# Moving mask making and two memsets on GpSimd, one first-layer group ahead of the first turn, and a fourth relu tile

## The chip, the cores and the metric

The kernel runs on one core of one Trainium2 chip. The metric is the device time of one execution in microseconds, as the median of several runs. The core has five engines with queues of their own: TensorE (PE, with its weight loads as PEld), VectorE (DVE), ScalarE (ACT), GpSimd (POOL) and SyncE (SP), which here issues the transfers.

## The reference

Sliding-window attention over q, k, v of shape (8, 8, 576, 64), then a two-layer feed-forward with a squared relu:

```python
scores = (q @ k.T) / sqrt(64); masked to |i - j| <= 32
attn = softmax(scores) @ v                       # (8, 8, 576, 64)
x = attn.transpose(0, 2, 1, 3).reshape(4608, 512)
r = max(x @ w_in, 0)                             # w_in  (512, 2048)
out = (s * r * r + b) @ w_out                    # w_out (2048, 512)
```

All inputs and the output are float32.

## The kernel before

The kernel interleaves attention, batch by batch, with the feed-forward, token block by token block. It casts to bf16 on the way in and multiplies in bf16.

**Order.** Nothing is issued in the order of the source. Each `add(...)` makes a task with an engine, an estimated cost, what it reads and writes, and a key. `plan()` then goes through a simulated schedule and always takes the task that can start first by the estimates, ties going to the lower key and then to the one created earlier. `emit()` writes the engines' queues in that order, with semaphore waits. On the chip each queue runs strictly in that order. The source order still counts, since a ring's tile is handed out in the order of creation, and so fixes who waits for whom.

**Start.** Batch 0's q and k come by pairs of heads into the eight staging tiles `STG` (`load_pair`, L662), are cast to bf16 (`cast_qk`, L687), turned by TensorE into one of the two PSUM banks `W` (`turn_pair`, L700), and copied out as `qt` (ACT, L705) and `kt` (DVE, L706). GpSimd makes the identity and `NEG`, an additive band that opens batch 0's score banks (`opened`, L957), with `affine_select` (`band`, L482 and L487).

**Weights.** `w_in` and `w_out` come in eight tiles each through the same `STG` ring (L550) and are cast by GpSimd (L553). The loads of batch 1's q and k reuse the ring behind the `w_out` tiles, so SP issues each of them when a `w_out` cast is done.

**Masks.** Batches from 1 on multiply the exponentials by `MASK` (L987, L838). `masks()` makes it with four `affine_select`s, then makes three variants from it, each a copy (L517) and one or two memsets (L520), used from batch 3 on. `colsum()` needs two tiles set beforehand (L1180, L1181); it forms the column sums of `w_out` for the term with b (TensorE L1182, DVE L1186, TensorE L1189, DVE L1191).

**First layer.** Token blocks 0, 1 and 2 have 96, 256 and 160 tokens. Their first layer is cut into groups (block, quarter of the 2048 hidden columns). `s1` runs a group into a `W` bank (L1119), ACT applies relu into one of `NR1` tiles `R1` (L1126), DVE squares it into `GT` (L1128). A group of block 0 takes one bank, a group of blocks 1 or 2 takes two, in turn. `FIRST` orders the groups and the four `TURN`s, in each of which one pair of heads of batch 1 is turned through the same two banks and its scores are issued. The last turn also brings the remaining rows and the first unit of batch 1.

**Second layer.** `early()` runs the second layer of the first four 128-token tiles in pieces as hidden columns become ready (L1168); later tiles run in `s2` (L1137). DVE forms the output (L1153), SP stores it.

Of the kernel before, what the change touches and what calls it, by code (L numbers as in the profile page):

```python
# [19 lines left out]
NUNIT = (NTILE + 1) // 2  # L20
# [10 lines left out]
WINE = ("pool", "pool", "pool", "pool")  # L31
TURNKEY = -17.5
TURN = (None, 0)
FIRST = ((0, 0), (1, 0), (0, 1), (1, 1), (2, 0), (2, 1), (0, 2), (1, 2), (2, 2), TURN, (0, 3), TURN, (1, 3), TURN, (2, 3), TURN)
WOUTE = (("pool", "pool"),) * 4
TAIL = ("act", "dve")
HOST = (("k", 3), ("q", 0))
# [289 lines left out]
def bass_sliding_window_symmetric__then__act_starrelu_kernel(  # L327
# [23 lines left out]
    with ExitStack() as es:  # L351
# [16 lines left out]
            uid["n"] += 1  # L368
            return es.enter_context(nc.psum_tensor(f"{nm}_{uid['n']}", list(shape), dt))

        NSTG, NNAT, NEX, NXN, NR1, NOUT, XR = 8, 6, 5, 5, 3, 5, 2048
        WIN_BF = sb((128, 4, DFF), BF16, "win")
        WOUT_BF = sb((128, 16, DM), BF16, "wout")
        XT = sb((128, NPAIR, XR), BF16, "xt")
# [14 lines left out]
        MASK = MASKS[0]  # L389
# [7 lines left out]
        ONESW = sb((128, 128), BF16, "onesw")  # L397
# [5 lines left out]
        OUTS = [sb((128, DM), F32, "outs") for _ in range(NOUT)]  # L403
# [17 lines left out]
        g = _Graph(queues)  # L421
        add = g.add
# [27 lines left out]
        def number(c, u):  # L450
            return c * NUNIT + u
# [41 lines left out]
        band(IDENT[:, :], ONESW[:, :], "IDENT", 0, 0, -98)  # L493
        for p0 in (0, 64):
            band(NEG[p0:p0 + 64, :], NEG[p0:p0 + 64, :], ("NEG", p0), 0, 64, -97, -FAR, source=("NEG", p0))
        ones = ONESW.rearrange("p (one c) -> p one c", one=1).to_broadcast((128, 4, 128))
        add("pe", [lambda e: e.matmul(W[:, 1, :].rearrange("p (a c) -> p a c", a=4), lhsT=ONESW[:, :], rhs=ones,
                                      start=True, stop=True)] * WARM,
# [12 lines left out]

        def masks(after):

            for p0 in (0, 64):
                band(MASK[p0:p0 + 64, :], ONESW[p0:p0 + 64, :], ("MASK", 0, p0), 0, 64, -24.0, waits=[after])
            for i, cuts in ((1, ((0, 96), (64, 0))), (2, ((64, 96),)), (3, ((0, 0),))):
                add("pool", lambda e, i=i: e.tensor_copy(MASKS[i][:, :], MASK[:, :]), 250,  # L517
                    reads=[("MASK", 0, 0), ("MASK", 0, 64)], writes=[("MASK", i, 0), ("MASK", i, 64)], key=0.0)
                for p0, c0 in cuts:
                    add("pool", lambda e, i=i, p0=p0, c0=c0: e.memset(MASKS[i][p0:p0 + 64, c0:c0 + WIN], 0.0), 150,  # L520
                        writes=[("MASK", i, p0)], key=0.0)
        for i in range(2):
            for c0 in (0, WIN + S):
                zero("dve", QT[i][:, :, c0:c0 + WIN], ("QTZ", i, c0), 150, key=-98 if i == 0 else -20)
            add("dve", lambda e, i=i: e.memset(VB[:, i * NUNIT:i * NUNIT + NUNIT, :, :].rearrange("p t h c -> p (t h) c")[:, :, D:D + 1], 1.0), 150,
                writes=[("VBO", i)], key=-57 if i == 0 else -20)
# [3 lines left out]
        land = {}  # L530
# [53 lines left out]
        def cast_v(c, u, key, eng, slack):  # L584
            vs, vb, n = number(c, u) % NUNIT, number(c, u) % (2 * NUNIT), 64 * len(tiles(c, u))
            add(eng, (lambda e: e.copy(VB[0:n, vb, :, 0:D], VST[0:n, vs, :, :])) if eng == "act" else
                (lambda e: e.tensor_copy(VB[0:n, vb, :, 0:D], VST[0:n, vs, :, :])),  # L587
                {"act": 617.0, "dve": 420.0, "pool": 750.0}[eng],
                reads=[("VST", vs)], writes=[("V", vb, y) for y in (0, 1)], key=key, slack=slack)

        def load_rows(y, load_key):

# [426 lines left out]
        def attention():  # L1019
            seq = {"k": -200.0}  # L1020

            def nxt():
                seq["k"] += 1.0
                return seq["k"]

            def w(which, i):
                for x in (0, 1):
                    load_weights(which, i, x, nxt(), WINE[i] if which == "in" else WOUTE[i][x])

            for pr in range(NPAIR):  # L1030
                for name in "qk":
                    load_pair(0, name, pr, nxt())
                    turn_pair(0, name, pr, -60.0 + 0.1 * pr, banks, K0[pr] if name == "k" else Q0[pr], 200.0)
                pair_scores(0, pr)
            pick()
            for name, t in ORDER0:
                if name == "v":
                    load_tail(nxt())
                elif name == "r":
                    load_rows(t, nxt())  # L1040
                elif name == "e":
                    load_rest(0, nxt(), REST[0], -26.5, 200.0)
                else:
                    w("in", t)
            place_v()
            turn_rest(0, -23.9, banks)
            place_tail()
            last_scores(0)
            first_units()
            masks(land["av", 0, NUNIT - 1])  # L1050
            for i, src in enumerate((moe_s, moe_b)):
                add("sp", lambda e, i=i, src=src: e.dma_start(SROW[0:128:32, i:i + 1], src.partition_broadcast(4)),
                    600.0, writes=[("SROW", i)], dma=("l", 1, 15.0), key=nxt())
            add("dve", lambda e: e.stream_shuffle(SB128[:, :], SROW[:, :], [0] * 32), 150,
                reads=[("SROW", 0), ("SROW", 1)], writes=[("SB128", 0), ("SB128", 1)], key=P2[0] - 8.0, slack=500.0)
            for step in ORDER1:
                if step[0] == "w":
                    w("out", step[1])
                elif step[0] == "v":
                    load_v(1, step[1], nxt(), "sp", [land["rows", y] for y in (0, 1)])  # L1060
                    cast_v(1, step[1], due(1, 0) - 4.0 + step[1], EV1[step[1]], 800.0)
                elif step[0] == "e":
                    load_rest(1, nxt(), REST[1], due(1, 0) - 1.4, 500.0)
                else:
                    for name in "qk":
                        load_pair(1, name, step[1], nxt())
            yield S
            for pr in range(NPAIR):
                if pr:
                    yield S  # L1070
                for name in "qk":
                    turn_pair(1, name, pr, TURNKEY + 0.1 * pr, banks, "dve" if name == "k" else "pool", 500.0)
                pair_scores(1, pr)
            turn_rest(1, due(1, 0) - 1.4, banks)
            last_scores(1)
            for u in range(NUNIT):
                last.append((1, u))
                close()
                yield closed[0]
            for b in range(PAIRS, B):  # L1080
                c = seq_of(b)
                later(b, due(c, group_of(b)[0]) - 24.0)
                for i, u in enumerate(group_of(b)):
                    load_v(c, u, due(c, u) - 35.0, late(b), [paced(b, PACEV[min(b, 4) - 2][i])])
                    cast_v(c, u, due(c, u) - 4.0, EV2[i], SLACK[3])
                for u in group_of(b):
                    unit(c, u)
                    yield closed[0]
            if seq_tiles(LONG) % 2 == 0:
                unit(LONG, seq_units(LONG) - 1)  # L1090
            while last:
                close()
            yield T
# [81 lines left out]

        def colsum():

            even, block = OUTS[NOUT - 2][:, 0:128], OUTS[NOUT - 1][:, :]
            made = [land["av", 0, NUNIT - 1]]
            add("pool", lambda e: e.memset(even, 1.0 / 32), 150, writes=[("OUTS", NOUT - 2)], key=-19.0, waits=made)  # L1180
            add("pool", lambda e: e.memset(block, 0.0), 500, writes=[("OUTS", NOUT - 1)], key=-19.0, waits=made)  # L1181
            add("pe", [lambda e, fc=fc, x=x: e.matmul(  # L1182
                SC[32 * x:32 * x + 32, 0, 0:128], lhsT=ONESW[:, 0:32], rhs=WOUT_BF[:, fc, 128 * x:128 * x + 128],
                start=(fc == 0), stop=(fc == 15)) for fc in range(16) for x in range(4)],
                1100, reads=["ONESW"] + [("Wout", i, x) for i in range(4) for x in (0, 1)], writes=[("SC", 0)], key=-12.0)
            add("dve", [lambda e, x=x: e.tensor_copy(block[32 * x:32 * x + 32, 128 * x:128 * x + 128],  # L1186
                                                     SC[32 * x:32 * x + 32, 0, 0:128]) for x in range(4)],
                800, reads=[("SC", 0)], writes=[("OUTS", NOUT - 1)], key=-12.0)
            add("pe", lambda e: e.matmul(SC[:, 1, :], lhsT=even, rhs=block, start=True, stop=True),  # L1189
                950, reads=[("OUTS", NOUT - 2), ("OUTS", NOUT - 1)], writes=[("SC", 1)], key=-12.0)  # L1190
            add("dve", lambda e: e.tensor_scalar(CVEC[:, :], SC[:, 1, :], SB128[:, 1:2], None, ALU.mult),  # L1191
                680, reads=[("SC", 1), ("SB128", 1)], writes=[("CVEC", x) for x in (0, 1)], key=P2[0])

        units, made = attention(), 0
# [5 lines left out]

        made = next(units)
        colsum()
        for m, i in FIRST:
            if m is None:
                made = next(units)
# [268 lines left out]
```

## Time and profile before

| what | value |
|---|---|
| time, median of 3 runs | 316.41 us (315.55 to 317.66) |
| profiled execution | 318.05 us, span 316.3 us |
| mean granted TensorE clock | 0.987 |
| TensorE busy | 303.9 us of the span |
| VectorE, ScalarE, GpSimd busy | 194.8, 141.9, 91.7 us |
| HBM read, written | 36.70 MB, 9.44 MB |

The span is the part of the profiled execution between its first and its last instruction; the rest of its time lies around it. The busy time of an engine says what it did, not whether anyone waited for it. For that one reads a stretch of the span by itself, and in it the wait that ended last.

### The profile page before, as it was taken

How to read it: one execution, taken by the hardware profiler on the slowest of the kernel's cores; microseconds unless marked ns; L12 is line 12 of the kernel's file. 1: busy time of each engine (PE TensorE's matmuls, PEld its weight loads, DVE VectorE, ACT ScalarE, POOL GpSimd, SP SyncE). 2: the span in 40 equal slices, each digit the busy share in tenths (PEclk: the TensorE clock that was granted, in tenths of full speed). 3: DMA queues.
4: the chain of work that ended last, by engine and by line, in shares of the span. 5: the costliest groups of instructions: out<-in, count | busy, mean ns of one | idle time of the engine just before them, and what ended most of it. 6: DMA issues, size and time to landing. Idle time of an engine off the chain costs nothing.

```text
span 316.3 us, 7961 instructions
## 1 busy us (share of the span) xinstructions
PE 303.9 (96%) x3348; PEld 161.6 (51%) x3348; DVE 194.8 (62%) x387; ACT 141.9 (45%) x224; POOL 91.7 (29%) x110
## 2 busy tenths in 40 slices
PE   6888969999999999999999999999999999999995
PEld 2466656567664454544444444444444444444444
DVE  4666465895897897795577576967445543333312
ACT  4746326356544775654265435444444333333300
POOL 3468973670406136131513411451000000000000
PEclk9799979999999999999999999999999999999999
DMA  6999999998994998799799799996221110000022
GB/s 214 330 380 388 360 229 241 225 188 296 248 182 137 297 166 164 242 206 153 184 290 151 149 251 313 167 169 157 64 63 51 52 46 33 35 35 33 36 96 74
DMA packets 100055, 56.10 MB, mean 177 GB/s; under 512 B 72048, under 2 KB 91248, under 8 KB 100016
## 3 DMA queue, kind: packets, MB, share of 16 engines
q1 hardware_dynamic: 100016, 55.56, 73.0%
q8 instruction: 27, 0.44, 0.6%
q14 instruction: 12, 0.10, 0.1%
HBM read 36.70 MB, written 9.44 MB: 146 GB/s over the span
## 4 chain that ended last, share of the span: by engine, by line
PE 83%; DMA 5%; POOL 4%; SPq 3%; DVE 3%; issue 1%; POOLq 0%
PE w L1119 36%; PE o L1137 35%; PE avn L864 4%; DMA stg<-in_moe_w_in_dram 4%; POOL wout L553 3%; PE sc L806 2%; DMA stg<-in_v_dram 1%; PE avn L1168 1%; SPq L662 1%; PE o L1168 1%; DVE outs L1153 1%; PE w L700 1%; PE avn L897 1%; SPq L673 1%; DVE vb L587 1%
## 5 line engine op out<-in xcount | busy, mean ns | idle before, releaser
L1119 PE MATMUL w<-xt,win 128*128 128x512 bf16 (+3 forms) x768 | 144.8, 327 | 1.1 <-issue 0.6
L1126 ACT ACTIVATE r<-w 128x512 bf16<-128x512 f32 (+2 forms) x148 | 86.6, 586 | 104.0 <-PE w L1119 87.6
L1137 PE MATMUL o<-wout,gt 128*128 128x512 bf16 (+1 forms) x528 | 126.8, 373 | 0.3 <-DVE gt L1128 0.3
L1128 DVE TENSOR_TENSOR gt<-r 128x512 bf16<-128x512 bf16 (+2 forms) x148 | 77.2, 526 | 75.9 <-ACT r L1126 75.5
L1119 PEld LDWEIGHTS w<-xt,win 128*128 128x128 bf16 x768 | 67.7, 98 | 53.9 <-issue 0.8
L1137 PEld LDWEIGHTS o<-wout,gt 128*128 128x128 bf16 x528 | 50.7, 98 | 55.8 <-DVE gt L1128 0.6
L755 POOL CAST nat<-stg 128x1024 bf16<-128x1024 f32 (+1 forms) x21 | 26.6, 1265 | 64.4 <-DMA stg<-in_q_dram 42.5
L772 POOL COPY kt<-ktr 128x512 bf16<-128x512 bf16 (+1 forms) x30 | 31.1, 1037 | 37.4 <-DMA ktr<-nat 35.9
L834 ACT ACTIVATE ex<-sc 128x1024 bf16<-128x1024 f32 (+1 forms) x28 | 28.6, 1023 | 22.5 <-PE avn L864 21.7
L1153 DVE SCALAR_TENSOR_TENSOR outs<-o,sb,cvec 128x512 f32<-128x512 f32 (+1 forms) x35 | 25.4, 728 | 11.4 <-PE o L1137 11.3
L890 DVE TENSOR_TENSOR xn<-avn,rec 128x512 bf16<-128x512 f32 (+1 forms) x31 | 21.3, 688 | 1.0 <-DVE rec L888 0.2
L838 DVE TENSOR_TENSOR ex<-ex,mask 128x1024 bf16<-128x1024 bf16 (+1 forms) x28 | 21.2, 757 | 1.1 <-ACT ex L834 0.5
L864 PE MATMUL avn<-vb,ex 64*64 64x65 bf16 x944 | 19.9, 197 | 0.3
L864 PEld LDWEIGHTS avn<-vb,ex 64*64 64x64 bf16 x944 | 12.9, 106 | 13.2 <-issue 7.8
L755 DVE CAST nat<-stg 128x1024 bf16<-128x1024 f32 (+1 forms) x15 | 12.2, 810 | 3.7 <-DMA stg<-in_k_dram 1.9
L587 DVE CAST vb<-vst 128x512 bf16<-128x512 f32 (+1 forms) x28 | 13.8, 494 | 0.8 <-DMA vst<-in_v_dram 0.7
L888 DVE RECIPROCAL rec<-avn 128x8 f32<-128x8 f32 (+1 forms) x31 | 6.2, 201 | 8.3 <-PE avn L864 8.0
L806 PE MATMUL sc<-qt,kt 64*64 64x128 bf16 x432 | 11.3, 216 | 0.0
L700 PE MATMUL w<-ident,nat 128*128 128x128 bf16 x64 | 7.0, 253 | 3.9 <-POOL nat L687 3.4
L905 ACT COPY xt<-avn 128x512 bf16<-128x512 bf16 (+2 forms) x14 | 7.1, 516 | 6.3 <-PE avn L897 6.3
L705 ACT COPY qt<-w 128x512 bf16<-128x512 bf16 x8 | 4.7, 584 | 11.3 <-PE w L700 11.3
L553 POOL CAST win<-stg 128x1024 bf16<-128x1024 f32 x8 | 8.6, 1080 | 3.6 <-DMA stg<-in_moe_w_in_dram 3.4
(119 smaller groups left out, 156.8 us busy)
## 6 DMA issues: line engine op xcount, KB each, us to landing
out_dram<-outs SPq DMA_DIRECT2D x35, 256.0 KB, 2.6
vst<-in_v_dram SPq DMA_DIRECT2D x28, 256.0 KB, 4.4
stg<-in_k_dram SPq DMA_DIRECT2D x6, 1024.0 KB, 10.6
stg<-in_q_dram SPq DMA_DIRECT2D x6, 1024.0 KB, 6.4
stg<-in_moe_w_in_dram SPq DMA_DIRECT2D x8, 512.0 KB, 9.3
stg<-in_moe_w_out_dram SPq DMA_DIRECT2D x8, 512.0 KB, 10.3
stg<-in_q_dram SPq DMA_DIRECT2D x8, 256.0 KB, 5.3
stg<-in_k_dram SPq DMA_DIRECT2D x8, 256.0 KB, 5.1
```

The source lines that it names most:

```text
L553: add(eng, (lambda e: e.copy(dst, stg)) if eng == "act" else (lambda e: e.tensor_copy(dst, stg)), {"act": 1040.0, "dve": 690.0, "pool": 11 ...
L755: add(eng, lambda e, x=x: e.tensor_copy(nat[0:top, 1024 * x:1024 * x + 1024].rearrange("p (i h d) -> p h i d", h=H, i=2), stg[0:top, :].re ...
L772: add("pool", lambda e, c=c, w=w: e.tensor_copy(KT[slot][:, :, c:c + w].rearrange("p a (s i) -> p a s i", i=4), KTR[slot][:, :, :, c // 4: ...
L834: add("act", lambda e, dst=flat_dst, src=flat_src: e.activation(dst, src, AF.Exp, bias=0.0, scale=0.125), 190 + 0.833 * 512 * len(hs), rea ...
L838: add("dve", lambda e, flat=flat, mask=mask: e.tensor_tensor(flat, flat, mask, ALU.mult), 130 + 0.53 * 512 * len(hs), reads=[("E", ei, hp, ...
L864: return [lambda e: e.matmul(av[64 * x:64 * x + 64, h, 0:D + 1], lhsT=buf[64 * g:64 * g + 64, h % 2, h // 2, c:c + 64], rhs=VB[64 * g:64 * ...
L890: add("dve", lambda e: e.tensor_tensor(XN[xi][0:p1, :].rearrange("p (a c) -> p a c", a=H), av[0:p1, :, 0:D], REC[ri][0:p1, :].rearrange("p ...
L1119: add("pe", [lambda e, g=g, kc=kc: e.matmul(wt[:, g, :], lhsT=WIN_BF[:, kc, (f0 + g) * 128:(f0 + g + 1) * 128], rhs=XT[:, kc, t0 % XR:t0 % ...
L1126: add("act", lambda e: e.activation(rt, wt, AF.Relu, bias=0.0, scale=1.0), 190 + 0.833 * ng * nt, reads=[("W", wb)], writes=[("R1", rb)], ...
L1128: add("dve", lambda e: e.tensor_tensor(GT[gs][:, f0:f0 + ng, g0:g0 + nt], rt, rt, ALU.mult), 130 + 0.53 * ng * nt, reads=[("R1", rb)], wri ...
L1137: add("pe", [lambda e, fc=fc: e.matmul(O[:, ob, 0:cn], lhsT=GT[gs][:, fc, g0:g0 + 128], rhs=WOUT_BF[:, fc, c0:c0 + cn], start=(fc == 0), s ...
L1153: add("dve", lambda e: e.scalar_tensor_tensor(OUTS[us][:, 0:cn], bank, SB128[:, 0:1], CVEC[:, c0:c0 + cn], ALU.mult, ALU.add), 200 + 1.07 ...
```

## The change

The four selects that make `MASK` and the two memsets of `colsum()` no longer wait for batch 0's last attention unit; they get keys that put them right behind `NEG`, at the start of the kernel. The three variants of the mask now wait for the last V cast of batch 1. In `FIRST`, group (0, 3) stands ahead of the first turn, and so each later group stands one turn earlier, with turns 2 and 3 together at the end. `R1` gets a fourth tile.

```diff
-FIRST = ((0, 0), (1, 0), (0, 1), (1, 1), (2, 0), (2, 1), (0, 2), (1, 2), (2, 2), TURN, (0, 3), TURN, (1, 3), TURN, (2, 3), TURN)
+FIRST = ((0, 0), (1, 0), (0, 1), (1, 1), (2, 0), (2, 1), (0, 2), (1, 2), (2, 2), (0, 3), TURN, (1, 3), TURN, (2, 3), TURN, TURN)
...
-        NSTG, NNAT, NEX, NXN, NR1, NOUT, XR = 8, 6, 5, 5, 3, 5, 2048
+        NSTG, NNAT, NEX, NXN, NR1, NOUT, XR = 8, 6, 5, 5, 4, 5, 2048
...
+        for p0 in (0, 64):
+            band(MASK[p0:p0 + 64, :], ONESW[p0:p0 + 64, :], ("MASK", 0, p0), 0, 64, -96)
+        even, block = OUTS[NOUT - 2][:, 0:128], OUTS[NOUT - 1][:, :]
+        add("pool", lambda e: e.memset(even, 1.0 / 32), 150, writes=[("OUTS", NOUT - 2)], key=-95.0, waits=[g.tasks[-1]])
+        add("pool", lambda e: e.memset(block, 0.0), 500, writes=[("OUTS", NOUT - 1)], key=-95.0, waits=[g.tasks[-1]])
...
         def masks(after):
-            for p0 in (0, 64):
-                band(MASK[p0:p0 + 64, :], ONESW[p0:p0 + 64, :], ("MASK", 0, p0), 0, 64, -24.0, waits=[after])
             for i, cuts in ((1, ((0, 96), (64, 0))), (2, ((64, 96),)), (3, ((0, 0),))):
                 add("pool", lambda e, i=i: e.tensor_copy(MASKS[i][:, :], MASK[:, :]), 250,
-                    reads=[("MASK", 0, 0), ("MASK", 0, 64)], writes=[("MASK", i, 0), ("MASK", i, 64)], key=0.0)
+                    reads=[("MASK", 0, 0), ("MASK", 0, 64)], writes=[("MASK", i, 0), ("MASK", i, 64)], key=0.0, waits=[after])
...
+            land["vb", c] = g.tasks[-1]          # in cast_v
...
-            masks(land["av", 0, NUNIT - 1])      # in attention, ahead of batch 1's loads
+            masks(land["vb", 1])                 # behind them
...
-            even, block = OUTS[NOUT - 2][:, 0:128], OUTS[NOUT - 1][:, :]
-            made = [land["av", 0, NUNIT - 1]]
-            add("pool", lambda e: e.memset(even, 1.0 / 32), 150, writes=[("OUTS", NOUT - 2)], key=-19.0, waits=made)
-            add("pool", lambda e: e.memset(block, 0.0), 500, writes=[("OUTS", NOUT - 1)], key=-19.0, waits=made)
```

## The prediction

> **What bounds the kernel now.** I read the page first, for which engine fills the span.
>
> ```profile
> span 316.3 us, 7961 instructions
> PE 303.9 (96%) x3348; PEld 161.6 (51%) x3348; DVE 194.8 (62%) x387; ACT 141.9 (45%) x224; POOL 91.7 (29%) x110
> ```
>
> TensorE is busy for 303.9 of 316.3 us, so at most 12.4 us of its idle time can be won, and GpSimd's 29% says nothing by itself. The next view is the busy time by stretch (after each stretch its length, then the busy time and instruction count of PE, PEld, DVE, ACT and POOL, the granted clock, the DMA share and GB/s).
>
> ```profile
> 28.00:42.00 14.00, 10.71 (x104) 7.42 (x102) 7.52 (x13) 4.86 (x11) 12.72 (x19) 1.00 1.00 344
> 42.05:45.45 3.40, 3.40 (x80) 3.01 (x81) 1.91 (x5) 0.66 (x2) 2.32 (x6) 0.50 0.96 229
> 45.45:60.00 14.55, 14.55 (x177) 8.82 (x174) 10.38 (x20) 8.73 (x14) 6.28 (x10) 1.00 1.21 249
> 60.00:80.00 20.00, 19.33 (x291) 13.70 (x291) 15.71 (x32) 9.70 (x18) 9.98 (x10) 1.00 1.02 234
> 80.00:250.00 170.00, 170.00 (x2001) 84.64 (x2000) 120.63 (x230) 85.39 (x128) 45.91 (x40) 1.00 0.83 176
> ```
>
> From 45.45 to 250 us TensorE lacks only 0.67 us of being full. What it has left to do at 42 us is a fixed amount of matmuls, so whoever lets it begin them earlier moves the end by as much. Between 28 and 42 us it idles 14.00 - 10.71 = 3.3 us, and there GpSimd is the full engine (12.72 of 14.00). After it, 3.4 us run at clock 0.50. The change edits this place. The chain that ended last, in order of time, says what holds it (start, length, what):
>
> ```profile
> 16.43 11.58 DMA stg<-in_moe_w_in_dram
> ...
> 28.13 1.26 POOL win L553
> ...
> 29.47 0.37 POOL mask L482
> ...
> 31.00 0.30 POOL mask L487
> ...
> 32.45 0.21 POOL outs L1180
> ...
> 33.93 0.54 POOL outs L1181
> ...
> 36.80 0.37 POOL mask L517
> ...
> 38.33 0.12 POOL mask L520
> ...
> 38.51 0.13 POOL mask L520
> ...
> 39.79 0.29 POOL mask L517
> ...
> 40.14 1.05 POOL wout L553
> 41.19 0.05 issue
> 41.24 0.69 POOL nat L687
> 41.99 0.99 PE w L700 x8
> 42.97 1.83 PE sc L1182 x64
> 44.80 0.54 PE w L700 x4
> 45.34 0.81 PE w L1119 x16
> ```
>
> Up to 28 us the chain is the transfer of the first weights. From 28.13 to 41.94 it is GpSimd alone, eight casts of the second weights with mask and memset instructions between them, and then the cast of batch 1's first q (L687), for which the first turn's transposes wait. The timeline shows that wait on TensorE, and DVE's wait for k:
>
> ```profile
> 41.99 0.99 PE L700 MATMUL w<-ident,nat 128*128 128x128 bf16 x8 [2.42 <-POOL nat L687]
> ...
> 40.21 1.25 DVE L687 CAST nat<-stg 128x512 bf16<-128x512 f32 x1 [1.76 <-DMA stg<-in_k_dram]
> ```
>
> TensorE stands still for 2.42 us, waiting for GpSimd. DVE's cast of the first k waits for its transfer, which lands at 40.2.
>
> **The change part by part.**
>
> **1. Mask and memset work leaves the GpSimd chain.** The eight quoted rows between 29.47 and 40.08 sum to 2.33 us; each has about 0.05 us of issue beside it, so some 2.8 us leave the chain. Not all of that comes out, because the transfers are behind it. The last second-layer weight tile is issued at 29.4 and such a tile takes 9.5 us to land (issues of 28 to 46 us):
>
> ```profile
> L550 SPq DMA_DIRECT2D stg<-in_moe_w_out_dram x8: 367/368/435, 18.2 to 29.4; - x8
> ...
> stg<-in_moe_w_out_dram SPq DMA_DIRECT2D x2, 512.0 KB, 9.5
> ```
>
> So it lands near 38.9, an estimate from these two rows. The DMA share is 1.00 over 28 to 42, so I let nothing land earlier. GpSimd, now waiting for transfers, then casts that tile (1.05) to 39.95 and q (0.69) to 40.7 with the gaps; q was issued ahead of the k that lands at 40.2. The first transposes start near 40.8 in place of 41.99: **1.2 us**. Bounds: 0, where q's or k's transfer sets the turn (k's cast ends at 40.21 + 1.25 = 41.46, and if its transposes stand ahead of other work they allow about 0.5), and 2.8, where the tile has long landed. I take the value nearest to the rows of transfers. The loads of batch 1 that follow each cast on the SP queue are issued earlier by at most as much and fill a queue that is already busy; I give that nothing.
>
> **2. Group (0, 3) ahead of the first turn.** Its 16 matmuls now stand behind the turn (0.81 in the chain, the first part at half clock). Its weights are cast by 28.13 + 1.26 = 29.4, and its bank is W1, which group (2, 2) leaves free at about 37, so it runs before TensorE goes idle and fills part of the 2.42. At full clock I take **0.7 us**; bounds 0.4 (half of 0.81) and 0.8. The W banks' sequence behind it changes, (1, 3) ahead of turn 1, (2, 3) ahead of turn 2, turns 2 and 3 together: turn 1's transposes now wait for the relu of (1, 3) and hold up what stands behind them on TensorE, where turn 2 did so before. The sum of the work doesn't change.
>
> **3. The clock.** The slow stretch is a consequence of the gap, by these stretches (PE alone: length, busy, clock, DMA):
>
> ```profile
> 4.52:7.94 3.42, 1.98 (x30) 1.00 0.97 293
> 7.94:11.35 3.41, 3.03 (x29) 0.50 1.09 366
> 28.40:31.80 3.40, 2.53 (x31) 1.00 1.05 383
> 38.65:42.05 3.40, 0.98 (x6) 1.00 0.80 244
> ```
>
> The two half-clock stretches (the second is the row from 42.05 above) are 3.41 us long and start 34.1 us apart, ten times that length, so I read them as steps of a fixed grid: a step busy for 0.98 or 1.98 of 3.4 is followed by a slow one, a step busy for 2.53 is not. With parts 1 and 2 the step from 38.65 has 0.98 + 0.7 + about 1.2 = 2.9 us of work and the next stays fast. What a fast one saves is bounded by 0 and by half of 3.40, 1.7. Piece by piece, with full-clock rows of the chain:
>
> ```profile
> 47.89 0.22 PE w L700 x4
> ...
> 61.68 0.35 PE w L864 x16
> ```
>
> Twelve transposes take 0.99 + 0.54 and would take 0.66; the 64 column-sum matmuls take 1.83, 29 ns each, and at the 22 ns of the small L864 matmuls 1.4. That is 0.87 + 0.43 = **1.3 us**.
>
> The Trainium skill, "TensorE: Matmul & The Clock Gate", Part 1, has a free-running window of 3413 ns and says the clock is halved after at least one idle window. The length agrees with the 3.41 us here; that the window must be idle does not, as 0.98 us of work stood in it. By a fully idle window the 2.42 us gap would have cost nothing and the sum would be 1.9 us.
>
> **4. What arrives at the start.** Four selects and two memsets now stand ahead of GpSimd's first cast.
>
> ```profile
> 2.79 0.29 POOL L482 TENSOR_SCALAR_AFFINE_SELECT neg<-neg 64x128 bf16<-64x128 bf16 x1
> 3.22 0.29 POOL L487 TENSOR_SCALAR_AFFINE_SELECT neg<-neg 64x128 bf16<-64x128 bf16 x1
> 6.76 0.61 POOL L687 CAST nat<-stg 128x512 bf16<-128x512 f32 x1 [3.25 <-DMA stg<-in_q_dram]
> ```
>
> At 0.43 from start to start the selects add 1.7 us, the memsets 0.21 + 0.54 and gaps: done by about 6.1, inside the 3.25 us in which GpSimd waits for a transfer anyway. One select may slip ahead of the last NEG select and delay the bank's opening by 0.43; the next pair waits for the same transfer at 6.76, so I cost it at nothing (0.43 without that cover).
>
> **5. What arrives later.** The mask copies and their memsets (about 1.5 us by the rows above, some 2 with gaps) now stand behind the V casts of batch 1, where GpSimd waits anyway:
>
> ```profile
> 55.13 1.04 POOL L755 CAST nat<-stg 128x1024 bf16<-128x1024 f32 x1 [3.01 <-DMA stg<-in_k_dram]
> ```
>
> Nothing, then. What is queued behind them on GpSimd is batch 2's first cast, and for its k and q wait batch 2's scores. If the 3.01 us weren't there, all that would come 2 us later, and TensorE with it at most by as much.
>
> **6. Four relu tiles.** ScalarE may run one group further ahead of DVE. Where TensorE is full this earns nothing; in 60 to 80 us at most the 0.67 that it idles. I take 0.
>
> **Sum:** 1.2 + 0.7 + 1.3 = 3.2 us. The profiled execution took 318.05 us (span 316.3 and 1.75 around it), so it would take 314.85. It is 1.64 above the median 316.41 of the runs, and I take the 3.2 off the median: **313.2 us**. The case's own range is 312.2 to 314.2.
>
> **The rivals.**
>
> *The slow step isn't there in most runs.* The grid's phase need not be that of this one execution; a 2.42 us gap that is cut by a step's edge leaves two steps with more than 1.98 of work. The runs lie 2.1 us apart, which one slow step in some of them would make. Then part 3 falls out: 1.9 us, 314.5. Against it: the gap is 71% of a step, so most phases put most of it into one. The skill's free-running window (same page and part) says the same of the phase; no run here shows it.
>
> *The change doesn't shorten the chain.* The turn waits for k's transfer and cast, not for GpSimd's masks, and only the moved group counts: 0.7 us, 315.7. For it: k's cast ends at 41.46, 0.5 before the present start. Against it: TensorE has the column sums to do until then.
>
> *More than the gap.* The W1 bank now passes to turns 1 to 3 without (0, 3) between them, batch 1's scores come earlier, and the 0.67 us of 60 to 80 goes too: 3.9 us, 312.5. For it: nothing that TensorE runs there needs a later transfer than before. Against it: DVE has 15.71 of 20 us to do there.
>
> *Slower: turns 2 and 3 back to back lay batch 1's chain bare.* With no group between the last turns, each must wait for the copy out of its W bank: 0.22 of transposes, about 0.3 to the copy, the copy itself and 0.2 back.
>
> ```profile
> 48.15 0.69 DVE L706 COPY kt<-w 128x512 bf16<-128x512 bf16 x1 [0.33 <-PE w L700]
> 53.45 1.02 ACT L982 ACTIVATE ex<-sc 128x1024 bf16<-128x1024 f32 x1 [1.02 <-PE sc L939]
> ```
>
> That is 1.4 us for each of turn 2, turn 3 and the rest, 4.2, then two exponentials of 1.02 that the next scores wait for, and a slow step (1.3) after such a gap: 7.5 - 3.2 = 4.3 us slower, 320.7. It decides once fewer than some 4 us of second-layer matmuls are ready then. Against it: the stretch from 45.45 to 60 is full today (14.55 of 14.55), with the turns as well as the second-layer work in it.
>
> **How the numbers follow.** Forecast 0.50, no slow step 0.13, no shorter chain 0.09, more than the gap 0.13, slower 0.15. One per cent, 3.16 us, is about what a measurement of this kernel can tell from no change. The forecast lies on that bound: 0.27 of its 0.50 above it, 0.23 within. Faster by over 1%: 0.27 + 0.13 = 0.40. Within: 0.23 + 0.13 + 0.09 = 0.45. Slower: 0.15. The range runs from 311.6 (part 1's upper bound, with part of the rest) to 318.0, which leaves out most of the slower case and little else.
>
> **What would show it.** Right: no mask or memset instruction between GpSimd's weight casts and waits for transfers ahead of them; L687's q cast starting near 40.0; the 96-column group before the first L700 transposes, which start near 40.8 with under 1.2 us of idle ahead of them; clock 1.00 from 38 to 60. Wrong: a new idle of TensorE between 44 and 60, a slow step there, or column sums later than 42.

## The result and the profile after

The changed kernel took 316.0 us (median of 22 runs, 314.55 to 317.34), the kernel before 317.49 on the same chip (22 runs). The ratio is 0.995 [0.9932, 0.9968]: 1.6 us faster, half of the 3.2 us of the forecast. The profiled execution took 316.67 us. Its page (lines of the changed kernel stand 3 to 4 above those of before):

```profile
span 314.9 us, 7897 instructions
PE 296.3 (94%) x3304; PEld 159.9 (51%) x3348; DVE 195.4 (62%) x387; ACT 142.0 (45%) x224; POOL 93.8 (30%) x110
PEclk9999999999999999999999999999999999999999
```

Of 3348 matmul records 44 are missing here, so a PE idle of 0.2 us means nothing in this trace. The stretches that were shown of before:

```profile
28.00:42.00 14.00, 11.23 (x177) 8.71 (x179) 8.49 (x15) 5.47 (x12) 11.05 (x12) 1.00 1.05 361
42.05:45.45 3.40, 3.35 (x25) 2.31 (x24) 3.34 (x8) 1.38 (x3) 1.43 (x3) 1.00 1.01 217
45.45:60.00 14.55, 13.56 (x207) 8.00 (x209) 10.43 (x19) 7.17 (x11) 10.37 (x19) 1.00 1.04 233
```

GpSimd fell from 12.72 to 11.05 of the 14 us, and the half-clock stretch is gone. The chain shows what now holds the start:

```profile
16.16 11.42 DMA stg<-in_moe_w_in_dram
...
27.63 1.14 POOL win L556
...
28.79 9.61 DMA stg<-in_moe_w_out_dram
...
38.45 1.05 POOL wout L556
...
39.55 0.62 POOL nat L691
...
40.22 0.40 PE w L704 x4
```

A transfer of 9.61 us stands where seven casts and eight mask and memset instructions stood. The first transposes start at 40.22 in place of 41.99; some of this is luck, since the chain is 0.50 ahead at 27.63 already (28.13 before), ahead of anything that the change touches. TensorE's view:

```profile
36.92 0.84 PE L1123 MATMUL w<-xt,win 128*128 128x96 bf16 x16
37.60 1.03 PE L1172 MATMUL avn<-wout,gt 128*128 128x512 bf16 x4
40.22 0.40 PE L704 MATMUL w<-ident,nat 128*128 128x128 bf16 x4 [1.60 <-POOL nat L691]
```

Next, how far TensorE is ahead later on, by the same relus of ScalarE. Before, then after:

```profile
101.16 0.60 ACT L1126 ACTIVATE r<-w 128x512 bf16<-128x512 f32 x1 [1.14 <-PE w L1119]
...
197.39 0.60 ACT L1126 ACTIVATE r<-w 128x512 bf16<-128x512 f32 x1 [1.13 <-PE w L1119]
```

```profile
98.00 0.60 ACT L1130 ACTIVATE r<-w 128x512 bf16<-128x512 f32 x1 [1.14 <-PE w L1123]
...
196.24 0.60 ACT L1130 ACTIVATE r<-w 128x512 bf16<-128x512 f32 x1 [1.13 <-PE w L1123]
```

The lead is 3.16 us at 101 (3.17 at 72, by a relu at 72.48 and 69.31), and 1.15 at 197 and at the last relus (1.38 by the two spans). So 2 us are lost between 100 and 197 us, a stretch that the prediction had called full. Of TensorE's waits there two are longer than what a missing record can feign (who waited for whom, total, times, longest):

```profile
PE avn L868 <- DVE ex L842: 1.0, 1, 1.0
PE avn L868 <- POOL kt L776: 0.5, 1, 0.5
```

The first is the plainest, near 142 us. Before, VectorE then TensorE:

```profile
138.96 0.68 DVE L755 CAST nat<-stg 128x1024 bf16<-128x1024 f32 x1
...
140.57 0.92 DVE L838 TENSOR_TENSOR ex<-ex,mask 128x1024 bf16<-128x1024 bf16 x1
```

```profile
142.89 0.32 PE L864 MATMUL avn<-vb,ex 64*64 64x65 bf16 x16
```

After, VectorE then TensorE:

```profile
138.31 0.69 DVE L759 CAST nat<-stg 128x1024 bf16<-128x1024 f32 x1 [1.26 <-DMA stg<-in_k_dram]
138.92 1.26 DVE L1132 TENSOR_TENSOR gt<-r 128x512 bf16<-128x512 bf16 x1
...
140.22 1.40 DVE L759 CAST nat<-stg 48x1024 bf16<-48x1024 f32 x1
...
142.15 0.67 DVE L842 TENSOR_TENSOR ex<-ex,mask 128x1024 bf16<-128x1024 bf16 x1
```

```profile
142.88 0.31 PE L868 MATMUL avn<-vb,ex 64*64 64x65 bf16 x13 [0.97 <-DVE ex L842]
```

The same AV matmuls (attention times V) start at 142.89 and 142.88. The new order has put more feed-forward work ahead of them, so that alone doesn't say how much is lost: in a run shown below (`e13`), with the queues of the change and lighter loads, they start at 141.69. What is lost here is the wait, 0.97 us. VectorE's cast of batch 5's k stood waiting for its transfer, and the mask multiplication, for which TensorE waits, stood behind it in VectorE's queue. SP issued that load at 128.61 before and at 127.97 after:

```profile
128.61 0.58 SPq L747 DMA_DIRECT2D stg<-in_k_dram  x1
```

```profile
127.97 0.58 SPq L751 DMA_DIRECT2D stg<-in_k_dram  x1
```

It was issued 0.64 us earlier and landed later. GpSimd's first cast of it started at 137.48 before, and at 138.34 after (its row is in the last section):

```profile
137.48 1.28 POOL L755 CAST nat<-stg 128x1024 bf16<-128x1024 f32 x1 [2.87 <-DMA stg<-in_k_dram]
```

### The profile page after: what moved, and what is told of

Its sections match the earlier page's. It is cut to its first block, busy times and chain, and to the rows that moved or that the text cites. A ratio compares the mean times of both kernels' runs of the same rounds, so it can differ in the third digit from the quotient of the medians.

```text
span 314.9 us, 7897 instructions
## 1 busy us (share of the span) xinstructions
PE 296.3 (94%) x3304; PEld 159.9 (51%) x3348; DVE 195.4 (62%) x387; ACT 142.0 (45%) x224; POOL 93.8 (30%) x110
## 4 chain that ended last, share of the span: by engine, by line
PE 67%; DMA 20%; DVE 6%; issue 3%; SPq 1%; POOL 1%; ACT 1%
PE o L1141 30%; PE w L1123 27%; DMA stg<-in_k_dram 7%; DMA vst<-in_v_dram 4%; DMA stg<-in_moe_w_in_dram 4%; DMA stg<-in_moe_w_out_dram 3%; PE avn L868 3%; DMA ktr<-nat 2%; DVE gt L1132 2%; PE sc L810 1%; PE avn L1172 1%; SPq L666 1%; DVE nat L759 1%; PE o L1172 1%; DVE ex L991 1%
## 5 line engine op out<-in xcount | busy, mean ns | idle before, releaser
L1123 PE MATMUL w<-xt,win 128*128 128x512 bf16 (+3 forms) x749 | 140.0, 325 | 3.7 <-ACT r L1130 1.4
L1141 PE MATMUL o<-wout,gt 128*128 128x512 bf16 (+1 forms) x510 | 123.0, 372 | 2.0 <-issue 1.4
L1132 DVE TENSOR_TENSOR gt<-r 128x512 bf16<-128x512 bf16 (+2 forms) x148 | 76.3, 520 | 75.4 <-ACT r L1130 75.1
L776 POOL COPY kt<-ktr 128x512 bf16<-128x512 bf16 (+1 forms) x30 | 32.4, 1080 | 41.0 <-DMA ktr<-nat 39.6
L842 DVE TENSOR_TENSOR ex<-ex,mask 128x1024 bf16<-128x1024 bf16 (+1 forms) x28 | 22.0, 786 | 1.0 <-ACT ex L838 0.2
L590 DVE CAST vb<-vst 128x512 bf16<-128x512 f32 (+1 forms) x28 | 13.1, 473 | 0.0
L556 POOL CAST wout<-stg 128x1024 bf16<-128x1024 f32 x8 | 9.0, 1122 | 1.7 <-DMA stg<-in_moe_w_out_dram 1.3
L1172 PE MATMUL o<-wout,gt 128*128 128x512 bf16 x28 | 8.2, 380 | 1.2 <-POOL wout L556 1.0
```

The lines of the kernel that those rows point to most:

```text
L556: add(eng, (lambda e: e.copy(dst, stg)) if eng == "act" else (lambda e: e.tensor_copy(dst, stg)), {"act": 1040.0, "dve": 690.0, "pool": 11 ...
L776: add("pool", lambda e, c=c, w=w: e.tensor_copy(KT[slot][:, :, c:c + w].rearrange("p a (s i) -> p a s i", i=4), KTR[slot][:, :, :, c // 4: ...
L842: add("dve", lambda e, flat=flat, mask=mask: e.tensor_tensor(flat, flat, mask, ALU.mult), 130 + 0.53 * 512 * len(hs), reads=[("E", ei, hp, ...
L1123: add("pe", [lambda e, g=g, kc=kc: e.matmul(wt[:, g, :], lhsT=WIN_BF[:, kc, (f0 + g) * 128:(f0 + g + 1) * 128], rhs=XT[:, kc, t0 % XR:t0 % ...
L1132: add("dve", lambda e: e.tensor_tensor(GT[gs][:, f0:f0 + ng, g0:g0 + nt], rt, rt, ALU.mult), 130 + 0.53 * ng * nt, reads=[("R1", rb)], wri ...
L1141: add("pe", [lambda e, fc=fc: e.matmul(O[:, ob, 0:cn], lhsT=GT[gs][:, fc, g0:g0 + 128], rhs=WOUT_BF[:, fc, c0:c0 + cn], start=(fc == 0), s ...
```

## The experiments

Theory A: the start does all that was forecast, and the q and k loads of the later batches, with the casts that wait for them, take back what goes beyond some slack. Rivals: B, the changed order of the queues itself makes the stalls; C, the masks earn nothing and the moved group is the whole gain. Ratios are to the kernel before on the same chip, with 95% intervals.

### One part of the change at a time

`e1`: the change without the moved group and the fourth tile.

```diff
-FIRST = (... (2, 2), (0, 3), TURN, (1, 3), TURN, (2, 3), TURN, TURN)
+FIRST = (... (2, 2), TURN, (0, 3), TURN, (1, 3), TURN, (2, 3), TURN)
-        NSTG, NNAT, NEX, NXN, NR1, ... = 8, 6, 5, 5, 4, ...
+        NSTG, NNAT, NEX, NXN, NR1, ... = 8, 6, 5, 5, 3, ...
```

> Only the masks and the two memsets move; the order of the groups and the three relu tiles are those of before. The theories are these. A: the start of the change works in full (3.2 us by 72 us), but the transfers and casts of the later batches moved by much less, so TensorE can keep only what it gains up to a slack of some 1.2 to 2 us. B: the new order of the queues makes the stalls near 141 and 179 us, however far ahead TensorE is. C: the masks earn nothing, the moved group makes the whole gain. Under A the first transposes start near 40.5 in place of 42.0, the half-clock step goes, TensorE is some 2.5 us ahead at 72 us, and the end is 1.0 to 1.8 us earlier (ratio 0.994 to 0.997). Under B the order is almost that of before, nothing is given back, and the end is 2.5 us earlier (0.992). Under C 0 (1.000).

0.9942 [0.9913, 0.997]: the masks alone give the whole gain. `e2`: before, with the new `FIRST` alone.

> Only the order of the first-layer groups and turns changes. Under A the gap ahead of the first turn shrinks by 0.7 us, the slow step after it may stay, TensorE is 0.7 us ahead at 72 us and keeps it, since that is within the slack: ratio 0.998. Under B the new order makes the stalls of 1.05 and 0.6 us here too: 1.000 to 1.003. Under C it has the whole gain of the change: 0.995.

1.0011 [0.9981, 1.004]: the moved group alone earns nothing. C falls. Why it earns nothing is seen on TensorE in e1, whose `FIRST` is that of before:

```profile
37.62 1.03 PE L1172 MATMUL avn<-wout,gt 128*128 128x512 bf16 x4
38.48 1.03 PE L1172 MATMUL o<-wout,gt 128*128 128x512 bf16 x4
40.98 0.68 PE L704 MATMUL w<-ident,nat 128*128 128x128 bf16 x8 [1.47 <-POOL nat L691]
```

With the old `FIRST` a second-layer piece of four matmuls (L1172 at 38.48) stands last ahead of the turn. With the new one (the rows at 36.92 and 37.60 above) group (0, 3) has come in and this piece has gone behind the turn. Group and piece are equally long, and the idle is the same, 1.60 and 1.47 us.

`e3` and `e4`: the change with `NR1 = 3`, and before with `NR1 = 4`.

> The change with three relu tiles. Under A and C the fourth tile earns nothing and the ratio is the change's, 0.995, with TensorE 3.2 us ahead at 72 us. Under B the order differs a little, the stalls fall elsewhere, and the ratio lies anywhere from 0.990 to 1.000.

> Only the fourth relu tile. All three theories: 1.000 within 0.002. If it is off by more, the fourth tile changes the order of the queues by itself, and what it costs or earns is part of the change's sum, where the prediction had 0.

0.9945 [0.9912, 0.9978] and 1.0013 [0.9985, 1.0042]: the fourth relu tile is worth nothing, as forecast.

### Slack, and V's loads

`e5` and `e6`: some 1.8 us of TensorE work added near 48 us to before and near 43 us to the change.

```diff
-            add("pe", lambda e: e.matmul(SC[:, 1, :], lhsT=even, rhs=block, start=True, stop=True),
+            add("pe", [lambda e: e.matmul(SC[:, 1, :], lhsT=even, rhs=block, start=True, stop=True)] * 3,
```

> The kernel before with the float32 matmul that spreads the column sums (near 48 us) issued three times over, all queues in the same order: TensorE gets some 1.8 us more to do there. It was full from 45 us on, so under A and B alike the end is up to 1.8 us later, ratio 1.003 to 1.006.

> The changed kernel with the same matmul issued three times over (near 43 us), queues in the same order: 1.8 us more for TensorE. Under A (TensorE has run ahead of the later batches' transfers and waits for them) most of it is taken out of those waits: the end is 0 to 0.9 us later than the changed kernel's, ratio to before 0.995 to 0.998. Under B (the order of the queues makes the stalls) it is 1.8 us later, 1.000 to 1.001.

1.0044 [1.0019, 1.0068] and 0.997 [0.9947, 0.9994]. Before pays 1.4 of the 1.8 us; the change goes from 0.995 to 0.997, some 0.6 us, though the intervals overlap. That fits A.

`e7` and `e8`: V loads of the fourth and later batches bring two of eight heads (the first five full), in before and in the change.

> The kernel before with the V loads of the batches from the fourth on bringing two of eight heads (but for the first five, which fill the tiles), issue, waits and order the same; the rest of V is stale. It takes about a fifth of the transfers' packets out of the stretch from 95 to 220 us. Under A TensorE was the bound there and the end is the same to 0.5 us earlier, ratio 0.998 to 1.000. Under B the same.

> The changed kernel with the same lighter V loads. Under A the stalls near 141 and 179 us go, since the data come earlier, and the 3.2 us that TensorE is ahead at 72 us are kept: 1.0 to 2.0 us earlier than the changed kernel, ratio to before 0.989 to 0.992. Under B the casts still collide in the same order and the ratio stays at 0.995.

1.0011 [0.9979, 1.0042] and 0.9944 [0.9919, 0.997]. A's expectation for e8 was missed: V's bytes aren't what holds the lead back.

### Filling the gap without moving anything

`e9`: before, with one piece ahead of the turn issued six times.

```diff
-                        start=(fc == 0), stop=(fc == 15)) for fc in (f0, f0 + 1)],
+                        start=(fc == 0), stop=(fc == 15)) for fc in (f0, f0 + 1)] * (6 if (i, n) == (2, 1) else 1),
```

> The kernel before, with the last early second-layer piece ahead of the first turn issued six times (ten more 128x512 matmuls, about 2.2 us of TensorE work put into the gap in front of the first transposes; the piece is summed six times into its tile, so that tile's values are changed). Nothing is moved. If the half-clock step comes from the gap alone, the first transposes stay near 42 us, the granted clock stays at 1.00 through 42 to 45.5 us, and TensorE is 1.3 us ahead at 70 us (my price of the step). Theory A (the end takes over what is beyond 1 to 2 us of a lead): nearly all of the 1.3 us stays, ratio 0.995 to 0.998. Rival D: the extra matmuls don't keep the clock up or the transposes come later, then ratio 1.000 to 1.004.

1.0061 [1.0029, 1.0093]: slower, as rival D had it, yet not for D's reason. The clock stayed up from 42 us on, and the lead was 1.52 us at 72 us in the trace (0.7 of it was there before the gap, at the ninth relu). Then this, on VectorE and TensorE:

```profile
139.65 0.69 DVE L755 CAST nat<-stg 128x1024 bf16<-128x1024 f32 x1 [2.70 <-DMA stg<-in_k_dram]
...
142.04 0.92 DVE L838 TENSOR_TENSOR ex<-ex,mask 128x1024 bf16<-128x1024 bf16 x1
```

```profile
143.01 0.32 PE L864 MATMUL avn<-vb,ex 64*64 64x65 bf16 x16 [1.58 <-DVE ex L838]
```

The order of before, with a lead and none of the change, stalls at the same place: B isn't needed for the stalls. VectorE's casts of q and k wait 6.3 us for k loads in this trace, where before has 1.9. The load at 139.65 was issued at 128.06, 0.55 us earlier than in before, and landed 2.2 later.

### What in the loads takes the lead back

`e10` and `e11`: the later q and k loads no longer wait for the last V load of the batch before, in the change and in before.

```diff
-                      ([land["v", seq_of(b - 1), group_of(b - 1)[-1]]] if b > PAIRS or LATE == PAIRS else []))
+                      [])
```

> The changed kernel, whose later batches' q and k loads no longer wait for the last V load of the batch before (they go out as soon as their buffers are free). Theory A1: the lead of 3.2 us is given back because these loads keep their old times and the casts of k stand waiting for them on VectorE ahead of the masks; then the k loads of batches 3 to 6 are issued over 1 us earlier, the stalls of TensorE at 86 to 102, 141 and 179 us go, and the ratio is 0.989 to 0.992. Rival A2: the DMA queues are full there whatever the order, so loads issued earlier take as much longer or push V or the output stores back, and TensorE loses the time in another place: ratio 0.993 to 0.998, with stalls on V's side or on the stores.

> Control for the run above: the kernel before with the same wait dropped. TensorE has no stall of more than 0.7 us in all between 45 and 250 us there, so theory A1 expects nothing from it: ratio 0.998 to 1.002. Rival A2 (earlier loads collide with V and the stores) expects 1.000 to 1.006. If it is below 0.997, the wait also costs the kernel before, and the gain of the run above is not the change's.

0.9998 [0.9958, 1.0038] and 1.002 [0.9994, 1.0047]. A1 (theory A, with the landing of the k loads as what takes the lead back) is wrong in this, and e10 came out worse than A2 had it: the wait was not the fault. In e10 batch 3's k load was issued 0.7 us earlier than in the change and batch 5's 1.3. But batch 4's was issued 0.6 us later and took 13.66 us instead of 11.94, and the stalls came in other places (chain of e10):

```profile
101.12 13.66 DMA stg<-in_k_dram
...
115.41 1.26 DVE gt L1132
116.67 1.44 DVE nat L759
```

So the load that took longest was not the one let out earliest. That fits A2, by one trace.

`e12`, `e15` and `e16`: casts of the later batches' q and k all on GpSimd, in the change (twice) and in before.

```diff
-CASTE = (("pool", "pool"), ("pool", "dve"))
+CASTE = (("pool", "pool"), ("pool", "pool"))
```

> The changed kernel with the k casts of the third and later batches on GpSimd, not VectorE: the loads keep their times, but a cast that waits for its load no longer stands ahead of a mask multiplication in VectorE's queue. If it is the place in VectorE's queue that turns a late load into a stall of TensorE (theory A1, its second half), the stalls at 86 to 102 and 141 us go and the ratio is 0.990 to 0.993. Rival A3: the late load itself is the bound (the transposes of k need it next), or GpSimd's casts (0.5 to 1.2 us each) become late themselves: ratio 0.994 to 1.000, with TensorE waiting for the transposes of k or for the score matmuls.

> The changed kernel with all casts of later batches' q and k on GpSimd, once more, for a closer interval. If a waiting cast on VectorE is what passes the late landing on to TensorE, pooled ratio 0.990 to 0.993 and no piece of the chain of waits on a k load; if it makes no difference, 0.994 to 0.996 as the changed kernel itself.

> Control for the run above: the kernel before with the casts of later batches' q and k on GpSimd. With TensorE 3 us later than in the changed kernel the loads have landed when the casts come: theory A1 expects 0.998 to 1.001. If it is below 0.997, casts on GpSimd are better whatever the start, and the gain of the run above is not the lead's.

0.9935 [0.9895, 0.9976], 0.9964 [0.993, 0.9998], and before 1.0004 [0.9977, 1.0031]. Taken together the first two lie where the change itself lies. Within the intervals the place of the cast makes no difference. So VectorE's queue is one way by which a late load reaches TensorE and not the bound: e15's chain has the load, GpSimd's casts and the transposing transfers in line.

```profile
156.15 11.52 DMA stg<-in_k_dram
167.73 1.04 POOL nat L759
...
170.95 6.95 DMA ktr<-nat
177.95 1.04 POOL kt L776
```

`e13` and `e14` go at the loads themselves: those of q and k made light, each engine's order unchanged.

```diff
-                stg[p0:p0 + n // 4, :].rearrange("p (h c) -> p h c", h=H),
-                src_of[name][b, :, t0:t0 + n, :].rearrange("h (p i) d -> p h (i d)", i=4))
+                stg[p0:p0 + n // 4, :].rearrange("p (h c) -> p h c", h=H)[:, 0:H if b < 3 else 2, :],
+                src_of[name][b, 0:H if b < 3 else 2, t0:t0 + n, :].rearrange("h (p i) d -> p h (i d)", i=4))
```

> The changed kernel, whose q and k loads of batches 3 to 7 (the fourth batch on) bring two of the eight heads, a quarter of the bytes; the other heads' values are left over from earlier batches. Casts, transposes and matmuls are all there, and the order on every engine is the same. Theory A1 (the landing of the k loads gives the lead back): they land several us earlier, no cast on VectorE waits for them, the stalls at 86 to 102, 141 and 179 us are gone, the lead of about 3.2 us at 100 us reaches the end, ratio 0.987 to 0.991. Rival A2 (other transfers, the transposing ones or V's, are late in their place, or the engines' order itself takes the lead back): ratio 0.992 to 0.996, with stalls left at the same places.

> Control: the kernel before with the same lighter q and k loads (two of eight heads from the fourth batch on). Its TensorE waits little for them: theory A1 expects 0.997 to 1.000 (the 0.7 us that it lacks in all between 45 and 250 us at most). If this is at 0.993 or less, the kernel before pays for the loads too, and the run above says less of the change.

0.988 [0.9838, 0.9922] (6 runs) and 0.997 [0.9941, 0.9998]. By medians the change is worth 2.9 us with light loads (313.99 against 316.89), close to the 3.2 of the forecast, and in e13's trace a lead over before of 2.98 us at 72 is 2.94 at 197. The later casts on VectorE in before, in the change and in e13 (count, busy time, mean ns, then the idle ahead of them and what ended most of it):

```profile
L755 DVE CAST nat<-stg 128x1024 bf16<-128x1024 f32 (+1 forms) x15 | 12.2, 810 | 3.7 <-DMA stg<-in_k_dram 1.9
```

```profile
L759 DVE CAST nat<-stg 128x1024 bf16<-128x1024 f32 (+1 forms) x15 | 12.7, 844 | 3.4 <-DMA stg<-in_k_dram 2.3
```

```profile
L759 DVE CAST nat<-stg 128x1024 bf16<-128x1024 f32 (+1 forms) x15 | 10.1, 676 | 0.0
```

VectorE waited for loads about as long before (3.7 us) as after (3.4). What the lead changed is that TensorE stood behind that wait: between 72 and 250 us the list of waits shows none of TensorE for before, and for the change those of 1.0 and 0.5. In e13 VectorE's wait and TensorE's are both nil. The windows from 73 to 87 and 127 to 141 us show the transfers of the change, then of e13:

```profile
73.00:87.00 14.00, 13.74 (x199) 10.12 (x200) 9.17 (x19) 8.82 (x14) 3.06 (x2) 1.00 1.11 265
127.00:141.00 14.00, 13.52 (x200) 7.00 (x202) 10.06 (x21) 8.34 (x13) 4.15 (x3) 1.00 1.02 227
```

```profile
73.00:87.00 14.00, 14.00 (x201) 10.12 (x200) 9.56 (x20) 8.81 (x14) 3.19 (x3) 1.00 0.63 185
127.00:141.00 14.00, 14.00 (x203) 6.86 (x202) 11.55 (x22) 8.25 (x12) 2.79 (x3) 1.00 0.55 116
```

The DMA share falls from 1.11 and 1.02 to 0.63 and 0.55, and TensorE is full there. (What the change lacks of 14.00 in these two rows is about what its one and two missing records are worth, so they don't show a stall.) Before has shares of 1.05 and 0.97 in the same windows without a stall: there TensorE comes 2 to 3 us later, and the full queues cost it nothing. So the bytes of the later q and k loads take the lead back, and issuing the loads earlier (e10) did not help. Light loads also leave more room for V and for the transposing transfers; e8 speaks against V, but whether k's landing or the transposing transfer behind it binds (as in e15) is not taken apart.

`e17` and `e18`: e9 and e1 with the same light loads.

> The kernel before with ten more matmuls in the gap ahead of the first transposes (as e9; that tile's values are changed) and with the lighter q and k loads of the fourth and later batches (two of eight heads, as e14). Theory A1: e9's lead of 1.5 us (0.8 of it the clock step) was turned into a loss by the casts that waited for the loads at 140 and 179 us; with light loads no such wait is left and the ratio is 0.991 to 0.995, some 1 us below e14's 0.997. Rival E: the extra matmuls themselves cost time or start later than the gap in most runs, then 0.998 to 1.004.

> Only the masks and memsets moved (as e1), with the lighter q and k loads. Theory A1: the lead of the first turn reaches the end, ratio 0.987 to 0.991. Against e13 (0.988, which has the moved group and the fourth relu tile too) this gives the moved group's own worth: if my 0.7 us (0.0022) for it was right, this is 0.990; if it was worth nothing, as the leads of 3.03 and 3.17 us in the two traces say, this is 0.988.

0.9963 [0.9941, 0.9986] and 0.9913 [0.9882, 0.9943] (6 runs). e17: the loss of e9 goes (1.0061 to 0.9963), so it was the loads that made it; but it is hardly better than e14 (0.9963 against 0.997), where A1 had wanted 1 us. It may be that the ten matmuls cost about what the clock step gives back; no run shows it. e18 lies beside e13 within the intervals, and these runs alone don't settle the moved group's worth.

The lead over before's trace at a relu of 72 us and at one of 197 shows the loads' part once more. With light loads it is kept: 2.98 and 2.94 in e13, 4.95 and 4.09 in e18 (4.09 from 80 us on; that one relu stands elsewhere in its order), 1.79 and 1.69 in e17. With full loads it shrinks: 3.17 to 1.15 in the change, 4.59 to 2.27 in e8, 4.19 to 2.16 in e15, 1.52 to -0.73 in e9. But not always: in e3's trace, with full loads, 5.08 us become 4.51, and TensorE has no wait over 0.2 us from 60 to 250. There batch 5's k load was issued at 125.26, 2.7 us earlier than in the change. So full loads took back a good part of the lead in most traces, and little in one.

### How often the slow step is there

The mean granted clock was recorded for every execution. A 3.4 us step at half clock lowers it over 315 us by 0.0054, so 0.994 is one step and 0.997 or more is none (the mean doesn't say where a step lay). Medians in us, with the number of executions; executions with a lower clock, two steps or more, are left out of the first two columns:

| kernel | no step | one step | executions counted |
|---|---|---|---|
| before, pooled over the experiments | 316.63 (48) | 317.42 (67) | 142 |
| changed | 315.62 (14) | 316.32 (3) | 22 |
| before, light q and k (e14) | 315.53 (3) | 317.20 (4) | 12 |
| changed, light q and k (e13) | 313.99 (6) | none | 6 |

A third of the executions of before (48 of 142) have no slow step, and of the changed kernel 14 of 22. Two traces show what else than the change decides. e14 has the gap, 2.44 us of it, and no slow step behind it (its one slow step lies at 10.5 us). e6 has the change and a slow step (after each stretch its length, the busy time of PE, PEld, DVE, ACT and POOL, then the clock, the DMA share and GB/s):

```profile
38.60:42.00 3.40, 0.96 (x9) 0.37 (x7) 1.10 (x1) 0.00 (x0) 3.08 (x6) 1.00 0.96 300
42.00:45.00 3.00, 3.00 (x95) 2.39 (x93) 2.54 (x8) 1.66 (x3) 2.25 (x5) 1.00 1.02 250
```

```profile
38.60:42.00 3.40, 1.08 (x34) 0.68 (x36) 0.81 (x2) 0.34 (x1) 2.51 (x4) 0.97 1.06 319
42.00:45.00 3.00, 3.00 (x59) 2.43 (x52) 2.06 (x6) 0.24 (x1) 1.40 (x3) 0.50 1.05 271
```

In e14 the steps of its grid, counted on from 10.5 by 3.41 us, begin at 37.8 and 41.2 us and cut the gap in two, with 1.5 and 2.9 us of work: that is the phase. The Trainium skill, "TensorE: Matmul & The Clock Gate", Part 1, calls the window free-running; e14 agrees with it. In e6 the phase is not the whole reason. Its last weight tile took 10.09 us where the change's took 9.61, and the gap was longer, 2.31 us in place of 1.60:

```profile
41.22 0.40 PE L704 MATMUL w<-ident,nat 128*128 128x128 bf16 x4 [2.31 <-POOL nat L691]
```

The table also gives the comparison that the forecast was about, an execution of before with one slow step against one of the changed kernel with none: 317.42 - 315.62 = 1.8 us with full loads, 317.20 - 313.99 = 3.2 with light ones (4 and 6 executions). At one clock state on both sides, none, it is 1.0 and 1.5.

## Why the prediction was right and wrong

The forecast of 313.2 us was taken off a median of three runs, 316.41; over 22 runs before has 317.49, so about 1.1 of the 2.8 us between 313.2 and 316.0 is the base. The rest is the gain, 1.6 us for 3.2.

**Part 1, GpSimd's chain: right.** No mask instruction is left between the weight casts, q's cast starts at 39.55 (forecast near 40.0), and the last weight tile landed at 38.4 (forecast near 38.9; it took 9.61 us for 9.5). The transposes start 1.77 us earlier; without the 0.50 by which this execution was ahead already, that is 1.27, and the forecast was 1.2. The idle ahead of them is 1.60 us, where it said under 1.2; that is part 2. e1 shows that this part makes the gain.

**Part 2, the moved group: mis-sized, 0.7 against nothing.** The step that failed here is "it runs before TensorE goes idle and fills part of the 2.42". It does run there, but a second-layer piece of the same length left the gap for it. I had priced the group by its duration and not looked at what the planner would do with the rest. e2's 1.0011 confirms it; e18 is open on it.

**Part 3, the clock: the slow step is gone in the profiled pair, but not for the reason given, and its price was too large for the median.** The step from 38.65 was to have 2.9 us of work. This stretch has 1.80:

```profile
38.60:42.00 3.40, 1.80 (x75) 1.56 (x75) 1.54 (x5) 0.58 (x1) 2.19 (x4) 1.00 0.99 311
```

By the prediction's own rows a step with 1.98 was followed by a slow one, so the forecast's rule would have put a slow step here. That none came is luck as far as the rule goes. The step of e14 with 1.5 wasn't followed by one either; where the line lies, and whether busy time is what counts, stays open. The size was right for a trace: in e9 the same eight transposes, column sums and four transposes run at full clock, from 41.54 to 43.34, 1.80 us, where before took 3.14 (41.99 to 45.13). That is 1.34 for the 1.3 of the forecast. But I took the step to be there in all executions of before. It is missing in a third of them and still there in some of the changed kernel's. With ordinary loads an execution of before with one step is 0.8 us longer than one without (317.42 against 316.63), with light loads 1.7 (few executions). The rival "the slow step isn't there in most runs", to which I gave 0.13, is partly true.

**Parts 4, 5 and 6: right.** Mask copies now run at 52.5 to 54.5 us, and GpSimd's next cast still waits 0.42 us for its transfer, of 3.01 before: the cover held, narrowly. In the profiled execution TensorE has no slow step and no late column sums.

**The last step failed:** "From 45.45 to 250 us TensorE lacks only 0.67 us of being full ... so whoever lets it begin them earlier moves the end by as much." This is the step that cost most: the loads that TensorE's later work needs were given no term. TensorE was full because each later batch's data was there just in time; VectorE's casts waited 3.7 us for loads before already, and TensorE none. I looked at the DMA share only where it held the start ("I let nothing land earlier") and gave the loads behind it nothing, though the rows from 45.45 on show 1.21, 1.02 and 0.83. In the same clock states the gain is 1.8 us with full loads and 3.2 with light ones, so the bytes of the later q and k loads took back some 1.4. The interval of that difference is wide, for the light side has ten executions; the traces with light loads, which keep their leads, bear it out. That full DMA queues make the loads land late is read from the windows and fits e10, but e8, which took V's bytes out of the queues, kept no more of the gain; this last link stays open.

The rival "slower", turns 2 and 3 back to back, did not come: the lead is as large behind them, at 72 us, as the start had made it. No version that leaves nothing out beat the changed kernel measurably.

## What to carry to other kernels

An engine that is full over a long stretch says what bounds it at today's pace, not that a head start will reach the end. Ask for each transfer in that stretch when it lands and when its reader comes up: the smallest slack is all that an earlier start is sure to earn, unless the transfers move too. Before taking credit for work moved into a gap, look at what leaves the gap for it, and before taking a clock step's price from one trace, look at how many executions have the step.

## What the runs showed of the hardware

The same start takes a different time each time. e3's queues are those of the change up to there, yet its ninth relu came at 28.46 us in the profiled execution and at 29.51 in that of the change, 1.05 us apart, and its span is 311.9 us against 314.9. Between two traces the ends differ here by 3.0 us, more than this whole change is worth.

VectorE's instructions can take two to three times as long beside GpSimd's casts, and a late k load brings that about, since it releases casts on both engines. In the change, at 138 us, GpSimd:

```profile
138.34 2.73 POOL L759 CAST nat<-stg 128x1024 bf16<-128x1024 f32 x2 [3.90 <-DMA stg<-in_k_dram]
```

In that time VectorE's square takes 1.26 us (0.41 elsewhere) and its cast of 48 partitions 1.40 (a mean of 0.669 in e13). A late load isn't needed for it: before's square at 137.78 took 1.25 us beside the cast at 137.48, and over a whole kernel the squares are no faster in e13 (a mean of 542 ns, 513 in the change). The Trainium skill, "SBUF — State Buffer", section "SBUF: two separate sides", says that VectorE and GpSimd share a port pair as an exclusive lock, which some VectorE operations take, among them those with two inputs in SBUF, and that whichever comes second waits for the whole instruction. The durations agree in kind; no run here takes the two apart at this place.
